# Sliding-window attention and a SiLU feed-forward on one core: the order of all work from a list scheduler, q and k in rows of 1.5 KB, v in four transfers a batch

## The chip, the cores and the metric

The kernel runs on one core of a Trainium2 chip. The metric is the device time of one execution in microseconds (us). A core has five engines that run side by side, each through its own instructions in their fixed order: PE (TensorE, matmuls and transposes), DVE (VectorE), ACT (ScalarE), POOL (GpSimd) and SP (SyncE, which here only issues transfers). PE's weight loads are shown as an engine of their own, PEld. An instruction waits at the head of its engine's queue for semaphores of the others, and everything behind it waits with it. Transfers (DMA) are issued by SP, ACT or POOL and then move by themselves.

## The reference

Attention over 8 batches, 8 heads, 576 positions and 64 values per head, where each position sees itself and the 63 before it; its output, as 4608 tokens of 512 values, goes through a feed-forward layer of width 2048.

```python
    scores = scale * np.matmul(q, k.transpose(0, 1, 3, 2))
    rel = pos[:, None] - pos[None, :]
    mask = (rel >= 0) & (rel < window)            # window = 64
    attn = np.exp(scores - max) / sum
    attn_out = np.matmul(attn, v)
    x = attn_out.transpose(0, 2, 1, 3).reshape(B * S, H * D)
    h = x @ w_in                                  # 4608x512 @ 512x2048
    g = h * (1.0 / (1.0 + np.exp(-h)))
    out = g @ w_out                               # 4608x2048 @ 2048x512
```

## The kernel before

**Attention.** The work is cut into 32 units `u` (one batch, two heads) and each unit into three groups `g` of three blocks of 64 positions, 96 groups in all. For a unit, `load_qk` brings q and k as 32-bit rows of 512 bytes (two positions), `cast` rounds them to 16 bits, `transposes` turns them on PE (six small matmuls for q, six for k) and copies the result from PSUM into `qbd` (two copies, one per head) and `kt` (one copy); these copies are called lifts below. `load_v` brings v in three transfers a unit, rounded on the way, and `fix_v` makes with two DVE copies the second alignment that the odd blocks need; these are called shifts.

A group is a chain through three engines: `scores` (three matmuls, then Exp on ACT at L168, then the mask on DVE at L169), `values` (three matmuls at L177, whose 65th column per head gives the sum; then on DVE a reciprocal at L184 and two multiplications at L187, together called the norm), `to_bridge` (three matmuls at L199 that bring the result back to the layout that the next layer reads, and a copy to `bridge` on ACT at L202).

**Feed-forward.** Tokens are taken in nine tiles of 512. `mm1` is the first layer: 16 output parts with four matmuls each (L226), each part followed by Silu on ACT (L233). `mm2` is the second layer: four blocks of 128 tokens with 16 matmuls each (L250), a copy on DVE (L238) and a store (L240). A tile of `mm1` has 64 matmuls of 512 columns and so has one of `mm2`.

**What sets the order.** The order is written out by hand. `interleave` runs the feed-forward as a stream and puts a step of other work behind every so many matmuls: in `mm1` after every sixth matmul one `bring_in` step (transposes, lifts and shifts of a later unit), in `mm2` after every third matmul one attention step (scores of one group, values of the group two steps back, `to_bridge` of the group four back). Tile 0's first layer is split into columns 0 to 191 and 192 to 511. `beside` says how many groups go beside each tile, 84 over tiles 0 to 7 (batch 0's 12 groups come before). Casts are on POOL from unit 4 on, between its v transfers; the first units' are on DVE and ACT. Lifts are shared by DVE and ACT in a fixed way. SP issues the q and k loads of later units and the stores.

**Buffers.** Four PSUM banks belong to the attention (`at_ps`) and four to the feed-forward (`moe_ps`).

## Time and profile before

| | |
|---|---|
| median of 3 runs | 395.9 us (395.88 to 396.58) |
| the profiled execution's own time, its span | 396.35 us, 394.6 us |
| mean granted TensorE clock | 0.989 |
| PE busy | 329.4 us, 83% |
| DVE busy | 232.9 us, 59% |
| ACT busy | 206.3 us, 52% |
| POOL busy (casts and issues of transfers) | 133.4 us, 34% |
| read from HBM, written | 36.70 MB, 9.44 MB |

Busy times are averages over stages with different limits. In the page's 40 slices PE is idle in the first two, at 4 to 8 tenths in the next two and between 7 and 9 later on; DVE changes between 9 and 4 tenths in the same slices in which PE changes between 7 and 9, and is idle from about 360 us on. The DMA engines are at 9 tenths in the first six and a half slices and seldom busy later. The chain that ended last is PE for 51% of the span, DVE for 32%, ACT for 6%.

### The profile page before, as it was taken

To read this page: it belongs to the slowest core of one execution; us is meant where nothing else is said; L and a number is where in the kernel's file an instruction comes from. 1 tells how busy PE (TensorE), PEld (TensorE's weight loads), DVE (VectorE), ACT (ScalarE), POOL (GpSimd) and SP (SyncE) were. 2 spreads that over 40 slices of the span, in tenths; PEclk is the share of its full clock that TensorE was granted. 3 is DMA by queue.
4 is the path that set the end of the run, shared out by engine and by line. 5 is a ranking of instruction groups with operands and counts; after the bars stand their busy time and mean duration, and the time that the engine had idled before them with its cause. 6 is when DMAs were issued, how large, how long until landed. Compare 5 with 4: busy or idle time off the path is not lost.

```text
span 394.6 us, 6598 instructions
## 1 busy us (share of the span) xinstructions
PE 329.4 (83%) x2423; PEld 180.0 (46%) x2464; DVE 232.9 (59%) x596; ACT 206.3 (52%) x410; POOL 133.4 (34%) x185
## 2 busy tenths in 40 slices
PE   0046896999989997899779978998799889989995
PEld 0035773545454554354435543545355544454442
DVE  0467979967584649664984485539944790093011
ACT  2066775545842774367445752585357645742710
POOL 8756999123900029200950077004900000000000
PEclk9999899899999999999999999999999999999999
DMA  9999999129901916382646456723710001001002
GB/s 190 166 213 250 119 209 174 9 17 272 120 27 71 250 10 64 71 213 54 65 51 185 109 57 86 201 67 43 71 55 0 30 27 55 0 28 69 13 27 80
DMA packets 83935, 37.65 MB, mean 95 GB/s; under 512 B 40256, under 2 KB 78656, under 8 KB 83904
## 3 DMA queue, kind: packets, MB, share of 16 engines
q0 software_dynamic: 45568, 11.28, 29.0%
q1 hardware_dynamic: 38336, 25.96, 24.4%
q8 instruction: 19, 0.31, 0.3%
q14 instruction: 12, 0.10, 0.1%
HBM read 36.70 MB, written 9.44 MB: 117 GB/s over the span
## 4 chain that ended last, share of the span: by engine, by line
PE 51%; DVE 32%; ACT 6%; issue 5%; POOL 2%; DMA 2%; DVEq 0%; ACTq 0%; POOLq 0%
PE ps L226 28%; PE ps L250 15%; DVE obd L187 13%; DVE e L169 7%; DVE rc L184 4%; PE pst L136 4%; ACT L168 2%; DVE ot L238 2%; PE pv L177 2%; DMA vv<-in_v_dram 2%; ACT e L168 2%; DVE qbd L143 2%; ACT gt L233 1%; POOL vv L75 1%; DVE vv L151 1%
## 5 line engine op out<-in xcount | busy, mean ns | idle before, releaser
L250 PE MATMUL ps<-w_out_sb,gt 128*128 128x512 bf16 x551 | 141.5, 381 | 1.3 <-ACT gt L233 0.3
L226 PE MATMUL ps<-bridge,w_in_sb 128*128 128x512 bf16 (+2 forms) x624 | 135.2, 359 | 0.9
L233 ACT ACTIVATE gt<-ps 128x512 bf16<-128x512 f32 (+2 forms) x160 | 84.6, 555 | 46.8 <-PE ps L226 45.3
L75 POOL DMA_DIRECT2D vv<-in_v_dram x64 | 49.1, 773 | 131.4 <-PE pv L177 90.6
L226 PEld LDWEIGHTS <-w_in_sb 128*128 128x128 bf16 x640 | 58.8, 99 | 51.9 <-issue 0.8
L169 DVE TENSOR_TENSOR e<-e,mask 128x384 bf16<-128x384 bf16 x96 | 43.0, 452 | 49.5 <-ACT e L168 47.1
L187 DVE TENSOR_TENSOR obd<-pv,rc 64x192 bf16<-64x192 f32 x192 | 68.2, 355 | 4.6
L250 PEld LDWEIGHTS <-gt 128*128 128x128 bf16 x576 | 49.4, 98 | 41.1 <-issue 1.0
L168 ACT ACTIVATE e<-sp 128x384 bf16<-128x384 f32 x96 | 44.7, 491 | 33.9 <-PE sp L162 33.8
L238 DVE COPY ot<-ps 128x512 f32<-128x512 f32 x36 | 24.6, 690 | 55.9 <-PE ps L250 55.3
L202 ACT CAST bridge<-op 128x192 bf16<-128x192 f32 x96 | 30.6, 318 | 45.6 <-PE op L199 44.3
L177 PE MATMUL pv<-vv,e 128*128 128x130 bf16 x288 | 33.8, 228 | 11.9 <-DVE e L169 6.8
L144 ACT COPY qbd<-pst 64x576 bf16<-64x576 bf16 x32 | 20.3, 633 | 40.3 <-DVE qbd L143 40.3
L199 PE MATMUL op<-twoi,obd 128*128 128x64 bf16 x288 | 25.1, 197 | 17.9 <-DVE obd L187 15.5
L162 PEld LDWEIGHTS <-kt 128*128 128x128 bf16 x288 | 25.2, 104 | 24.0 <-issue 2.9
L136 PE MATMUL pst<-ident,q_natb 96*128 96x96 bf16 x192 | 14.4, 214 | 26.0 <-DVE q_natb L126 26.0
L162 PE MATMUL sp<-qbd,kt 128*128 128x128 bf16 x288 | 33.2, 231 | 3.1 <-ACT kt L147 1.4
L147 DVE COPY kt<-pst 128x576 bf16<-128x576 bf16 x28 | 21.1, 755 | 18.3 <-PE pst L136 18.3
L177 PEld LDWEIGHTS <-e 128*128 128x128 bf16 x288 | 21.9, 101 | 20.9 <-DVE e L169 10.8
L199 PEld LDWEIGHTS <-obd 128*128 128x128 bf16 x288 | 15.7, 99 | 33.2 <-DVE obd L187 32.8
L143 DVE COPY qbd<-pst 64x576 bf16<-64x576 bf16 x32 | 24.0, 749 | 11.1 <-PE pst L136 11.0
L126 POOL CAST q_natb<-q_nat 96x768 bf16<-96x768 f32 x28 | 24.7, 881 | 13.3 <-DMA q_nat<-in_q_dram 13.3
(37 smaller groups left out, 188.8 us busy)
## 6 DMA issues: line engine op xcount, KB each, us to landing
out_dram<-ot SPq DMA_DIRECT2D x36, 256.0 KB, 2.1
q_nat<-in_q_dram SPq DMA_DIRECT2D x28, 288.0 KB, 6.1
k_nat<-in_k_dram SPq DMA_DIRECT2D x28, 288.0 KB, 6.1
vv<-in_v_dram POOLq DMA_DIRECT2D x64, 64.0 KB, 3.3
w_in_sb<-in_moe_w_in_dram POOLq DMA_DIRECT2D x8, 256.0 KB, 7.5
w_out_sb<-in_moe_w_out_dram POOLq DMA_DIRECT2D x8, 256.0 KB, 7.1
q_nat<-in_q_dram POOLq DMA_DIRECT2D x4, 288.0 KB, 8.8
k_nat<-in_k_dram POOLq DMA_DIRECT2D x4, 288.0 KB, 9.0
```

What stands on the lines that cost most here:

```text
L75: nc.gpsimd.dma_start(out=t[:, 1:9:2, hh * 65:hh * 65 + 64], in_=v[b, 2 * pj + hh, 0:512, :].rearrange("(c p) d -> p c d", p=128),)
L143: copies[0](out=d[0:64, 0], in_=src[0:64])
L162: nc.tensor.matmul(sp[:, x], lhsT=kt[i][:, t * 64:t * 64 + 128], rhs=qbd[i][:, :, t * 64:(t + 1) * 64], start=(x == 0), stop=(x == 2),)
L168: nc.scalar.activation(out=e, in_=sp, func=ACTF.Exp, scale=scale)
L169: nc.vector.tensor_mul(e, e, mask0 if g == 0 else mask)
L177: nc.tensor.matmul(pv[:, x, :], lhsT=e[:, x].rearrange("p h i -> p (h i)"), rhs=vv[i][:, 3 * g + x, :], start=(x == 0), stop=(x == 2),)
L187: nc.vector.tensor_mul(ob[p0:p0 + 64, :, p0:p0 + 64], pv[p0:p0 + 64, :, hh * 65:hh * 65 + 64], rc[p0:p0 + 64, :, hh:hh + 1].to_broadcast([ ...
L199: nc.tensor.matmul(op[:, x, :], lhsT=ob[:, x, :], rhs=twoi, start=(x == 0), stop=(x == 2))
L226: nc.tensor.matmul(ps[:, lo:hi], lhsT=w_in_sb[:, c, ft * 128:(ft + 1) * 128], rhs=bridge[c][:, t0 + lo:t0 + hi], start=(c == 0), stop=(c = ...
L233: nc.scalar.activation(out=gts[(j, ft)][:, lo:hi], in_=ps[:, lo:hi], func=ACTF.Silu)
L238: nc.vector.tensor_copy(out=ot, in_=ps)
L250: nc.tensor.matmul(ps[m], lhsT=gts[(j, f)][:, m * 128:(m + 1) * 128], rhs=w_out_sb[:, f, :], start=(f == 0), stop=(f == NFT - 1),)
```

## The change

The hand-written order goes. Every piece of work is added to a `Plan` with its class, the engines that may do it with a duration for each, and what it depends on. `Plan.run` then goes through the pieces in a model of the engines: whenever an engine is free it takes, in the order of `rank`, the first class whose next piece has its inputs and (for PE) a free PSUM bank; the instructions are emitted in that order. A piece of the kinds cast, lift, bridge copy or output copy may go to ACT or DVE, whichever is free. Scores are let through by `scores_may_run` only while the second layer runs with more than six matmuls left, or while the first layer has not its inputs yet.

Besides, a row of q and k now holds six positions (1.5 KB; 96 rows by two heads), k of batch 0 is issued by ACT, and v comes once per batch in four transfers of nine 128-row pieces, all issued by POOL, with two shifts per batch over 64x36x64 elements in place of eight over 64x512. `qbd`, `kt` and `vv` are kept per batch, two of each. Casts leave POOL altogether: by the order below 29 are on ACT and 35 on DVE. Tile 0's first layer is no longer split (64 matmuls fewer). All 96 groups are done by the fourth matmul of tile 5: beside tiles 1 to 4 stand 72 `values`, 69 `scores`, 71 `to_bridge` and 39 transposes of one q or k; tiles 5 to 8 have the feed-forward alone, but for one `to_bridge`.

```diff
+                for e in engines:
+                    if free[e] > now:
+                        continue
+                    for c in can[e]:
+                        q = self.queues[c]
+                        if head[c] == len(q):
+                            continue
+                        op = q[head[c]]
+                        if e not in op["us"]:
+                            continue
+                        if not self.done(op["deps"]) or (op["gate"] and not op["gate"]()):
+                            continue
+                        if op["pool"]:
+                            ok = [i for i, u in enumerate(self.banks[op["pool"]]) if self.done(u)]
+                            if not ok:
+                                continue
+                            op["bank"] = min(ok, key=lambda i: max(
+                                [u["seen"] for u in self.banks[op["pool"]][i]], default=0.0))
+                            self.banks[op["pool"]][op["bank"]] = op["until"]
+                        head[c] += 1
+                        us = op["us"][e]
+                        if op["table"] and op["table"] != table:
+                            table, us = op["table"], us + 1.28
+                        end = free[e] = now + us
+                        if op["dma"] is None:
+                            op["seen"] = end + op["lat"]
+                        else:
...
+                            pipe = max(pipe, end + 0.6) + op["dma"]
+                            op["seen"] = pipe + 1.4
+                        order.append((op, e))
+                        op["at"], op["cls"], op["by"] = now, c, e
+                        left -= 1
+                        moved = True
+                        heapq.heappush(events, end)
+                        heapq.heappush(events, op["seen"])
+                        break
+        for op, e in order:
+            op["fn"](e)
...
+    nats = [keep.tile([NR, 2, NM * D], FP32, name=f"nat{i}") for i in range(NN)]
+    natbs = [keep.tile([NR, NM, 128], BF16, name=f"natb{i}") for i in range(NNB)]
+    qbd = [keep.tile([128, NP, 2, S], BF16, name=f"qbd{i}") for i in range(NK)]
+    kt = [keep.tile([128, 64 + NP * S], BF16, name=f"kt{i}") for i in range(NK)]
+    vv = [keep.tile([128, H * NB + 1, D + 2], BF16, name=f"vv{i}") for i in range(NK)]
...
-    def load_v(u):
-        b, pj = divmod(u, NP)
-        t = vv[u % NK]
-        for hh in range(2):
-            nc.gpsimd.dma_start(
-                out=t[:, 1:9:2, hh * 65:hh * 65 + 64],
-                in_=v[b, 2 * pj + hh, 0:512, :].rearrange("(c p) d -> p c d", p=128),
-            )
...
+    p = Plan(
+        {name: len(b) for name, b in banks.items()},
+        rank=["one", "silu", "norm", "exp", "mask", "pv", "ot", "s", "bridge", "lift", "turn", "moe", "out",
+              "shift", "cast", "st", "ld0", "ld1", "dma"],
+    )
...
+    def load_qk(e, i, b, pj, kk):
+        queue[e].dma_start(
+            out=nats[i],
+            in_=(q, k)[kk][b, 2 * pj:2 * pj + 2].rearrange("h (p m) d -> p h (m d)", m=NM),
+        )
+
+    def load_v(b, part):
+        g0, g1 = part * 9, part * 9 + 9
         nc.gpsimd.dma_start(
-            out=t[64:128, 8, :].rearrange("p (h x) -> p h x", h=2)[:, :, 0:64],
...
+    def cast(e, i, w):
+        copies[e](
+            out=natbs[w].rearrange("p m (h d) -> p h m d", h=2),
+            in_=nats[i].rearrange("p h (m d) -> p h m d", m=NM),
+        )
...
+    def turn(op, w):
...
+    def lift_q(e, op, b, pj, hh):
+        r = slice(64 * hh, 64 * hh + 64)
+        copies[e](
+            out=qbd[b % NK][r, pj, hh].rearrange("x (p m) -> x p m", m=NM),
+            in_=at_bf16(op)[r].rearrange("x (m p) -> x p m", m=NM),
...
+    def lift_k(e, op, b, pj):
+        copies[e](
+            out=kt[b % NK][:, 64 + pj * S:64 + (pj + 1) * S].rearrange("x (p m) -> x p m", m=NM),
+            in_=at_bf16(op).rearrange("x (m p) -> x p m", m=NM),
...
+    def shift_v(b, hf):
+        t = vv[b % NK]
+        if hf:
+            nc.vector.tensor_copy(out=t[0:64, 2:H * NB + 1:2, 0:D], in_=t[64:128, 1:H * NB:2, 0:D])
         else:
-            d = kt[u % NK][:, 64:64 + S].rearrange("x (g p c) -> x g p c", g=3, c=2)
-            copies[0](out=d, in_=src)
...
+    def scores_may_run():
+        i = next((i for i in range(scores_may_run.i, len(moe)) if moe[i][0]["seen"] is None), None)
+        if i is None:
+            return True
+        scores_may_run.i = i
+        op, kind, rest = moe[i]
+        if kind == 1:
+            return rest == NFT * NDC and not p.done(op["deps"])
+        return rest > 6
+    scores_may_run.i = 0
...
+                           [ld, natb_free.get(w)])
+                nat_free[i] = ca
+                tu = p.add("turn", {"PE": 0.27}, None, [ca, c_ident] + busy, lat=0.1, pool="at")
+                tu["fn"] = lambda _, tu=tu, w=w: turn(tu, w)
+                natb_free[w] = tu
+                if kk:
+                    li = [p.add("lift", {"ACT": 0.64, "DVE": 0.75},
+                                lambda e, tu=tu, pj=pj: lift_k(e, tu, b, pj), [tu] + busy)]
+                else:
+                    li = [p.add("lift", {"ACT": 0.64, "DVE": 0.75},
+                                lambda e, tu=tu, pj=pj, hh=hh: lift_q(e, tu, b, pj, hh), [tu] + busy)
+                          for hh in range(2)]
+                tu["until"] = li
+                kq_done[(b, pj)] += li
+
...
+    def add_batch_v(b):
+        busy = pv_last.get(b - NK, []) + [c_vv[b % NK]]
+        lv = [p.add("dma", {"POOL": 1.0}, lambda _, part=part: load_v(b, part), busy, dma=2.7) for part in range(4)]
+        v_done[b] = lv + [p.add("shift", {"DVE": 0.8}, lambda _, hf=hf: shift_v(b, hf), lv) for hf in range(2)]
+
...
+                          kq_done[(b, pj)] + g_pv[n - NE:n - NE + 1] * (n >= NE), lat=0.1,
+                          gate=scores_may_run, pool="at")
+                s["fn"] = lambda _, s=s, pj=pj, g=g: scores(s, b, pj, g)
+                s_last[(b, pj)] = [s]
+                ex = p.add("exp", {"ACT": 0.5}, lambda _, s=s, n=n: expo(s, n), [s], table="exp")
...
-                if c == NDC - 1:
-                    if lo == 0:
-                        gts[(j, ft)] = g_pool.tile([128, TT], BF16, name="gt", tag="g")
-                    nc.scalar.activation(out=gts[(j, ft)][:, lo:hi], in_=ps[:, lo:hi], func=ACTF.Silu)
-                yield
...
-    for j in range(NTT):
...
-        for u in nxt:
-            load_v(u)
-            cast(u, "q", pcopy)
-            cast(u, "k", pcopy)
+                ot = n_ot[0] % NOT
+                n_ot[0] += 1
+                cp = p.add("out", {"DVE": 0.7, "ACT": 0.62}, lambda e, bank=bank[m], ot=ot: copy_out(e, bank, ot),
+                           [op, free_ot.get(ot)])
+                bank[m]["until"] = [cp]
+                free_ot[ot] = p.add("st", {"SP": 0.45}, lambda _, ot=ot, m=m: store(ot, j, m), [cp], dma=0.75)
+        free_gt.update(uses)
```

**DVE at the start.** Before, the clears of the buffers stand ahead of the first cast; `qbd`, `kt` and `vv` are a unit's buffers, and the L121 clears wait for v's transfers (DMASW).

```order
L120 MEMSET vv_106 64x65
L121 MEMSET vv_106 128x18 [waits DMASW7_49,DMASW0_49,DVE_49]
L117 MEMSET kt_99 128x32
L118 MEMSET qbd_91 64x288
L119 MEMSET qbd_91 64x288
L120 MEMSET vv_107 64x65
L121 MEMSET vv_107 128x18 [waits DMASW3_49,DMASW2_49,DVE_49]
L288 COPY twoi<-ident 64x64 [waits Pool_49]
L289 COPY twoi<-ident 64x64
L290 COPY mask_86<-mask 128x384 [waits Pool_49]
L291 MEMSET mask_86 64x64 [waits DVE_49]
```

After, the clears of two batches' buffers come first, and then lifts (L239, L245), casts (L221) and the first mask (L276); `at` is an attention PSUM bank, `nat` the loaded and `natb` the rounded q or k.

```order
L178 MEMSET kt_86 128x32
L179 MEMSET qbd_84 64x4x288
L180 MEMSET qbd_84 64x4x288
L239 COPY qbd_83<-at_145 64x576 [waits Activation_49]
L221 CAST natb_79<-nat_69 96x2x6x64 [waits DMAHW3_49]
L221 CAST natb_81<-nat_71 96x2x6x64 [waits DMAHW5_49]
L239 COPY qbd_83<-at_148 64x576 [waits PE_49]
L239 COPY qbd_83<-at_148 64x576
L245 COPY kt_85<-at_145 128x576 [waits PE_49]
L276 TENSOR_TENSOR e_89<-e_89,mask_65 128x384 [waits DVE_49,Activation_49]
L221 CAST natb_82<-nat_72 96x2x6x64 [waits DMAHW4_49]
```

The wait for v has moved from the clears to the first shift, 21 rows behind the last row shown.

**DVE in the middle.** Before, around the change from a first layer to a second one: lifts and shifts of the last two units, then masks and norms.

```order
L143 COPY qbd_94<-pst 64x576
L147 COPY kt_102<-pst 128x576
L151 COPY vv_110<-vv_110 64x4x2x64
L152 COPY vv_110<-vv_110 64x4x2x64
L143 COPY qbd_95<-pst 64x576
L147 COPY kt_103<-pst 128x576
L151 COPY vv_111<-vv_111 64x4x2x64
L152 COPY vv_111<-vv_111 64x4x2x64
L169 TENSOR_TENSOR e<-e,mask 128x384 x3
L184 RECIPROCAL rc<-pv 128x6
L187 TENSOR_TENSOR obd_112<-pv,rc 64x3x64 x2
L169 TENSOR_TENSOR e<-e,mask 128x384
```

After, in tile 1 around the same change (L288 and L291 are the norm, `ob` its output):

```order
L221 CAST natb_79<-nat_69 96x2x6x64
L239 COPY qbd_84<-at_147 64x576 x2
L221 CAST natb_80<-nat_70 96x2x6x64
L221 CAST natb_81<-nat_71 96x2x6x64
L276 TENSOR_TENSOR e_102<-e_102,mask_65 128x384
L276 TENSOR_TENSOR e_89<-e_89,mask 128x384
L288 RECIPROCAL rc_106<-at_145 128x6
L291 TENSOR_TENSOR ob_110<-at_145,rc_106 64x3x64 x2
L288 RECIPROCAL rc_103<-at_146 128x6
L291 TENSOR_TENSOR ob_111<-at_146,rc_103 64x3x64 x2
L276 TENSOR_TENSOR e_90<-e_90,mask 128x384
```

The casts of q and k stand now on DVE among the lifts, and masks and norms are no longer one after another by a fixed pattern.

**POOL.** Before, from tile 0 on, casts and v transfers take turns:

```order
L126 CAST q_natb<-q_nat 96x2x6x64 [waits PE_49]
L126 CAST k_natb<-k_nat 96x2x6x64 [waits PE_49]
L75 DMA vv_104<-in_v_dram 128x4x64 [waits DMASW0_49,PE_49]
L75 DMA vv_104<-in_v_dram 128x4x64 [waits DMASW1_49]
L79 DMA vv_104<-in_v_dram 64x2x64 [waits DMASW2_49,PE_49]
L126 CAST q_natb<-q_nat 96x2x6x64 [waits DMAHW0_49,PE_49,Pool_49]
```

After, POOL has only transfers; the first four of the third batch, which wait for PE to have read the first batch's v:

```order
L202 DMA vv_87<-in_v_dram 128x9x64 [waits DMASW0_49,DVE_49,PE_49]
L202 DMA vv_87<-in_v_dram 128x9x64 [waits DMASW1_49,PE_49]
L202 DMA vv_87<-in_v_dram 128x9x64 [waits DMASW2_49,PE_49]
L202 DMA vv_87<-in_v_dram 128x9x64 [waits DMASW3_49,PE_49]
L202 DMA vv_88<-in_v_dram 128x9x64 [waits DMASW4_49,DVE_49,PE_49]
```

The casts have left this queue.

## Rows read from the trace of the kernel before

**Rows 1.** Stretches: us, PE, PEld, DVE, ACT, POOL busy, PEclk, DMA, GB/s.

```profile
40.00:45.00 5.00, 3.79 (x37) 3.49 (x36) 4.60 (x16) 2.90 (x8) 4.17 (x7) 0.66 1.64 140
210.00:220.00 10.00, 9.89 (x75) 5.33 (x75) 6.41 (x12) 6.95 (x12) 0.00 (x0) 1.00 0.93 239
230.00:240.00 10.00, 7.38 (x68) 4.09 (x67) 9.25 (x25) 4.11 (x11) 10.00 (x15) 1.00 0.79 73
```

**Rows 2.** Chain of waits in order of time: start us, us, what.

```profile
89.25 1.24 PE ps L226 x5
...
167.98 1.08 PE ps L226 x5
...
209.84 1.08 PE ps L226 x5
...
362.98 6.47 PE ps L226 x30
...
390.65 0.69 DVE ot L238
```

**Rows 3.** Timeline around 206 to 232 us: start us, us, engine, line, instruction.

```profile
210.76 0.42 PE L136 MATMUL pst<-ident,q_natb 96*128 96x96 bf16 x6
...
212.31 0.42 PE L136 MATMUL pst<-ident,k_natb 96*128 96x96 bf16 x6
...
213.74 0.29 DVE L152 COPY vv<-vv 64x512 bf16<-64x512 bf16 x1
...
230.65 0.33 PE L177 MATMUL pv<-vv,e 128*128 128x130 bf16 x3
...
230.82 0.25 PE L199 MATMUL op<-twoi,obd 128*128 128x64 bf16 x3
...
230.91 0.81 PE L250 MATMUL ps<-w_out_sb,gt 128*128 128x512 bf16 x3
```

**Rows 4.** DVE groups of 310 to 327 us, where POOL is idle.

```profile
L187 DVE TENSOR_TENSOR obd<-pv,rc 64x192 bf16<-64x192 f32 x22 | 7.8, 355 | 0.5
L169 DVE TENSOR_TENSOR e<-e,mask 128x384 bf16<-128x384 bf16 x8 | 2.9, 358 | 0.2
L184 DVE RECIPROCAL rc<-pv 128x6 f32<-128x6 f32 x11 | 2.1, 194 | 0.3
```

**Rows 5.** Groups of the whole span by line and shape: busy us, mean ns.

```profile
L233 ACT ACTIVATE gt<-ps 128x512 bf16<-128x512 f32 x128 | 73.3, 597 | 45.9 <-PE ps L226 45.1
...
L168 ACT ACTIVATE e<-sp 128x384 bf16<-128x384 f32 x96 | 44.7, 491 | 33.9 <-PE sp L162 33.8
L169 DVE TENSOR_TENSOR e<-e,mask 128x384 bf16<-128x384 bf16 x96 | 43.0, 452 | 49.5 <-ACT e L168 47.1
...
L202 ACT CAST bridge<-op 128x192 bf16<-128x192 f32 x96 | 30.6, 318 | 45.6 <-PE op L199 44.3
...
L143 DVE COPY qbd<-pst 64x576 bf16<-64x576 bf16 x32 | 24.0, 749 | 11.1 <-PE pst L136 11.0
...
L144 ACT COPY qbd<-pst 64x576 bf16<-64x576 bf16 x32 | 20.3, 633 | 40.3 <-DVE qbd L143 40.3
...
L126 ACT CAST k_natb<-k_nat 96x768 bf16<-96x768 f32 x4 | 3.3, 831 | 3.4 <-DMA k_nat<-in_k_dram 3.4
...
L168 ACT ACT_TABLE_LOAD x8 | 10.3, 1283 | 0.1
...
L118 DVE MEMSET qbd<- 64x288 f32 x8 | 2.4, 298 | 0.0
...
L126 DVE CAST q_natb<-q_nat 96x768 bf16<-96x768 f32 x4 | 2.1, 537 | 0.1
```

**Rows 6.** Timeline of the start.

```profile
12.66 0.61 POOL L79 DMA_DIRECT2D vv<-in_v_dram  x1
...
20.22 0.66 PE L136 MATMUL pst<-ident,q_natb 96*128 96x96 bf16 x6 [20.22 <-DVE q_natb L126]
```

**Rows 7.** DMA issues of 2 to 20 us, last number us to landing.

```profile
vv<-in_v_dram POOLq DMA_DIRECT2D x4, 16.0 KB, 7.2
```

## What I predict, and how the numbers come about

> **What bounds the kernel now.** I read the chain of waits first, for the times at which the tiles begin, then the stretches, then the timeline of single instructions for PE's own pace, then the groups by line for what DVE and ACT have to do.
>
> PE's own pace. Tile 8 has nothing beside it: its first matmul starts at 362.98 and its last output copy at 390.65 [rows 2], so 128 matmuls take 27.67 us, 0.2162 each. In the first layer two pieces of transposes stand 1.55 us apart with six matmuls between [rows 3], so six transposes cost 1.55 - 6 x 0.2162 = 0.25. In a second layer the values begin at 230.65, the way back to the layout at 230.82 and the next matmul at 230.91 [rows 3]: 0.17 and 0.09. Scores are three matmuls like the values; I give them 0.17 as well. A group is 0.43.
>
> All of PE's work at this pace: 1152 x 0.2162 + 64 x 0.25 + 96 x 0.43 = 249.1 + 16.0 + 41.3 = 306.4 us. The first of it starts at 20.22 [rows 6], and behind the last output copy's start 394.6 - 390.65 = 3.95 us pass. So 394.6 - 20.2 - 306.4 - 3.95 = 64 us are PE standing still or at its lower clock. They lie in three places. (1) Before 20.22, because the first cast stands behind DVE's clears, which wait for v. (2) In batch 0's attention and tile 0: tile 1 begins at 89.25 [rows 2]. (3) In the second layers: the tile from 167.98 to 209.84 [rows 2] takes 41.86 us, and its own work (27.7, twelve groups 5.2, eight transposes 2.0) is 34.9, so 7.0 are lost. The stretches show where: from 230 to 240 us DVE is busy 9.25 of 10 and PE 7.38, from 210 to 220 DVE 6.41 and PE 9.89 [rows 1]. The attention's DVE work is all put beside second layers and DVE is the limit there, while in first layers it has time to spare.
>
> **The change part by part.** The terms are the start of tile 0, the start of tile 1, tiles 1 to 4 with all the attention left, tiles 5 to 8 with none, and the end.
>
> *Start of tile 0.* DVE's clears no longer wait. They run from about 0.9 us (an estimate): four of 64x1152, four times the 0.298 of 64x288 [rows 5], are 4.8; some 16 small ones, none taken above the 0.29 of a 512-element copy [rows 3] and put at 0.2, are 3.2. Then the order gives DVE, ahead of the first shift, 8 lifts of 0.749, 7 casts of 0.537 [rows 5] and 13 masks of 0.358 [rows 4]: 6.0 + 3.8 + 4.7. That is 23.6 without waits; for waits on PE and ACT in the first chains I add 0.9: 24.5. ACT's share ahead of it (7 casts of 0.831, 9 lifts of 0.633, 13 Exps of 0.491, a table of 1.283 [rows 5]) is 19.2, less than DVE's, so DVE is later. v must have landed by 24.5. In before its last transfer is issued at 12.66 and takes 7.2 [rows 6, 7], so it lands at 20; I take v as hidden. The two shifts have 4.5 times the elements of one before: at most 4.5 x 0.29 [rows 3] = 1.3 each, which I take. 27.1, the values 0.5 behind, then twelve norms of 0.194 + 2 x 0.355 = 0.904 [rows 4] with small gaps, 11.3: 38.9. One lift and a copy to `bridge` (0.318 [rows 5]) stand behind: tile 0 begins at 40.0.
>
> *Start of tile 1.* Tile 0's first layer is 13.85 + five transposes 1.25. PE is thinly used until then, and in before the stretch in which it came into steady work, 40 to 45 us, was granted 0.66 of full speed [rows 1]: between its two levels, 1.2 and 2.4 GHz, which costs (1 - 0.66) x 5 = 1.7. So 56.8. ACT: last Silu 0.8, table 1.28, twelve Exps 5.9: 64.8. DVE follows with the masks (0.133 shorter each than an Exp, so 1.6 of the two shifts' 2.6 are hidden), the last mask, a lift and the first values: 67.3. Twelve norms end at 78.6; way back and copy 0.7. Tile 1 begins at 79.5. PE's work by then would end at 77.2, so it stands 2.3 us. Before it was 89.25: only 10 us are won here.
>
> *Tiles 1 to 4.* PE: 4 x 27.7 + 39 x 0.25 + (69 + 72) x 0.17 + 71 x 0.09 = 110.8 + 9.75 + 24.0 + 6.4 = 150.9. DVE, by the order's counts and [rows 3 to 5]: 72 norms 65.1, 69 masks 24.7, 27 lifts 20.2, 23 casts 12.4, 10 shifts 13.0, 10 copies to `bridge` 3.2, 2 outputs 1.4 (0.69 each [rows 2]) = 140.0. ACT: 64 Silus of 0.597 are 38.2, 69 Exps 33.9, 62 copies to `bridge` 19.7, 31 lifts 19.6, 15 casts 12.5, 14 outputs at a Silu's length 8.4, 8 tables 10.3 [rows 5] = 142.6. PE is the longest of three, but DVE has 93% and ACT 94% of its time: nothing stands still without someone else noticing. How much PE waits is the term that no row shows. It is nothing if the three fit into one another, and 0.16 us for each of PE's attention pieces if they wait as in the tile of 41.86 us (7.0 over 12 x 3 + 8 = 44 pieces): 251 pieces, 40 us. The nearer row is the first layer's stretch, where pieces stand beside a DVE that is not full and PE keeps 9.89 of 10 [rows 1]; DVE is fuller here, so I take 5%, 8 us.
>
> *POOL.* Its casts go. A mask takes 0.358 where POOL is idle [rows 4] and 0.452 over the whole span [rows 5]; I have used 0.358. The Trainium skill (SBUF — State Buffer, section "SBUF: two separate sides") says that VectorE and GpSimd share a pair of ports that one of them holds for a whole instruction while the other "fully blocks". The mask rows agree with it. By that rule the casts, which are now DVE's, could hold POOL up in turn when it issues v; v is wanted a batch later, so this alone would leave the sum as it is.
>
> *Rows of 1.5 KB, four v transfers.* I cost them at nothing from tile 1 on: the attention works one to two batches ahead, and the loads go with it. If that cover were gone, a q would show its landing time once; the start has that case below.
>
> *Tiles 5 to 8 and the end.* 4 x 27.7 = 110.8, and 3.95 behind the last copy's start.
>
> Sum of the span: 79.5 + 150.9 + 8 + 110.8 + 3.95 = 353.2. The profiled execution took 396.35 for a span of 394.6, and the median is 0.45 below it, so +1.75 - 0.45: 354.5 us, 10% less than 395.9.
>
> **The rivals.**
>
> *A. The fixed order locks.* A list that is written by a model puts each PE piece where its input is just ready. If the real input comes later, all of PE's queue waits. At the 0.16 us a piece of before, tiles 1 to 4 lose 40 us: 345.2 + 40 + 1.3 = 386.5. For it: DVE and ACT have 6 or 7% to spare. Against: a late piece shifts the rest of the list as well, so that the same delay is not paid again, and Silu and Exp back to back can only be quicker than I counted.
>
> *B. v comes late at the start.* For it: q is issued by SP, k by ACT and v by POOL, behind which w_in is queued at once, and the loads of batch 1 come early too. If v lands at 30 to 35 in place of 24.5, tile 0 and all behind it move by 5 to 11: 360 to 366. Against: the bytes ahead of v are the same as before. The Trainium skill (DMA: Bandwidth & Descriptors, section "Queues, rings and completion order") has each DMA engine go round the queue rows that have work for it. No run here shows three rows at work. By that rule v would get a third of the turns in place of half, and its landing at 20 would become at most 30 (an estimate, 20 x 1.5): tile 0 later by 5.5, and 360 in all.
>
> *C. Slower than before.* The same place as A, but waits longer than before's: no spare time is left in DVE and ACT, and a mask that is late delays values, norm, way back and copy one after another. The point from which it decides: (395.9 - 346.5) / 251 = 0.197 us a piece. At 0.25 the sum is 346.5 + 63 = 409. For it: in before there are two steps between a group's scores and its values, here as few as the model wants. Against: before already paid 0.16 with DVE over its limit, and here DVE's demand is below PE's.
>
> That the order is not the planned one is no rival: it is read from the built program.
>
> **How the numbers follow.** My forecast, 354.5 with PE's wait between 0 and 20 us, has 71%; A (waits of 20 to 45) 13%; B 11%; C 3%; 2% for a gain lost in some other way that leaves no change. The range reaches down to 342 (no wait in tiles 1 to 4 gives 346.5, and 4 us less if the clears and first chains pack better than I added) and up to 370, which takes in B and the forecast with 20 us of waits and leaves out A's upper part and C. Chances: faster by over 0.2% 0.95, within 0.2% 0.02, slower 0.03; 0.2% is about what a measurement of this kernel can tell from no change.
>
> **What would show it.** First transposes before 10 us instead of at 20.22; tile 0's first matmul at 40 and tile 1's at 79.5; no idle PE in four tiles of 27.7 us each at the end; DVE and ACT at 9 tenths between 80 and 235 us with PE at 9 as well; masks of 0.36 us throughout. Wrong would be: PE at 7 tenths between 80 and 235 (A or C), the first shift waiting for a transfer (B), tile 5 beginning later than 255 us.

## The result and the profile after

The changed kernel takes 357.65 us (median of 4 runs, 356.06 to 358.78) beside 396.24 for the kernel before in the same session: a ratio of 0.902, 95% interval 0.899 to 0.906. The forecast was 354.5 in a range of 342 to 370. The profiled execution took 357.72 for a span of 355.8.

The first part of the page of after gives busy time and share of each engine; the rows below it are two of the 40 slices' rows, in tenths.

```profile
PE 323.2 (91%) x2358; PEld 178.4 (50%) x2400; DVE 193.4 (54%) x516; ACT 230.0 (65%) x448; POOL 46.7 (13%) x57
...
PE   1554699998999999999999999999999999999995
...
DVE  7966861679868989999978997791000000000000
```

PE went from 83% to 91% of a shorter span, and from the sixth slice to the last but one it is at 9 tenths, with one 8; before it changed between 7 and 9. DVE has no work from the 29th slice on: the attention is over by then, and the last third is the feed-forward alone.

The chain of waits of after, in order of time (start us, us, what), answers [rows 2]:

```profile
5.99 22.47 DMA vv<-in_v_dram
28.58 0.76 DVE vv L255
...
45.33 3.19 PE mp L305 x7
...
88.41 3.18 PE mp L305 x14
...
241.26 0.65 PE mp L305 x3
...
351.97 0.58 ACT ot L320
```

It begins with v: a transfer issued at 5.99 that lands after 22.5 us, then the first shift, then tile 0 at 45.33. From 88.41 on the pieces are PE's nearly without a break, and behind the last output copy's start 3.83 us pass.

The stretch of tiles 1 to 4, which before showed what [rows 1] show (PE at 7.38 of 10 where DVE was at 9.25), with the same columns:

```profile
86.23:241.09 154.86, 152.38 (x1356) 89.15 (x1381) 133.05 (x364) 127.22 (x264) 16.00 (x16) 1.00 0.55 103
```

PE is busy 98% of it, DVE 86%, ACT 82%.

Where the kernels begin their tiles, read from the timeline (the first first-layer matmul of each tile, us), with the medians; the rows below before and after are the experiments of the next section, and each of their ratios is to before in the same session. Some orders leave groups for tile 5, so tile 6 is the point at which all the attention is done.

| kernel | tile 0 | tile 1 | tile 6 | tiles 1 to 5 | median |
|---|---|---|---|---|---|
| before | 41.46 | 89.25 | 288.75 (not done) | | 396.24 |
| after | 45.33 | 86.23 | 268.84 | 182.6 | 357.65 |
| e1_hold | 36.74 | 85.69 | 270.88 | 185.2 | 359.67 |
| e7_rows512 | 41.22 | 81.41 | 264.30 | 182.9 | 353.35 |
| e8_vunit | 42.00 | 78.74 | 267.36 | 188.6 | 355.48 |
| e5_poolcast | 44.80 | 94.85 | 289.43 | 194.6 | 378.54 |
| e3_pvgate | 47.06 | 87.46 | 269.48 | 182.0 | 357.46 |
| e9_fixed | 45.51 | 88.34 | 287.84 | 199.5 | 376.39 |
| e6_blind | 45.56 | 89.37 | 313.57 | 224.2 | 402.16 |
| e13_low15 | 44.60 | 84.31 | 279.21 | 194.9 | 367.79 |
| e14_high15 | 45.22 | 86.11 | 268.32 | 182.2 | 357.15 |
| e4_nogate | 45.04 | 86.45 | 271.62 | 185.2 | 361.41 |
| e12_best | 40.73 | 76.90 | 260.46 | 183.6 | 349.83 |

After begins tile 1 only 3 us ahead of before. The rest of the 38.6 us is won behind it: from tile 1 to the start of the last output copy pass 301.4 us before [rows 2] and 265.7 after. Two questions are left: why the start is no better than that (v late?), and what keeps PE fed beside tiles 1 to 4.

### The profile page after: what moved, and what is told of

It is laid out like the page before. It is cut to its first block, busy times and chain, and to the rows that moved or that the text cites. A ratio compares the mean times of both kernels' runs of the same rounds, so it can differ in the third digit from the quotient of the medians.

```text
span 355.8 us, 6294 instructions
## 1 busy us (share of the span) xinstructions
PE 323.2 (91%) x2358; PEld 178.4 (50%) x2400; DVE 193.4 (54%) x516; ACT 230.0 (65%) x448; POOL 46.7 (13%) x57
## 4 chain that ended last, share of the span: by engine, by line
PE 75%; DVE 9%; DMA 6%; ACT 4%; issue 2%; POOL 1%; another core or an unknown queue 1%; DVEq 0%; ACTq 0%; POOLq 0%
PE mp L314 31%; PE mp L305 30%; DMA vv<-in_v_dram 6%; DVE ob L291 4%; PE at L267 4%; PE at L281 4%; PE at L232 3%; PE at L296 2%; ACT qbd L239 2%; DVE qbd L239 2%; DVE rc L288 1%; ACT g L311 1%; POOL vv L202 1%; DVE natb L221 1%
## 5 line engine op out<-in xcount | busy, mean ns | idle before, releaser
L314 PE MATMUL mp<-w_out_sb,g 128*128 128x512 bf16 x553 | 142.9, 379 | 0.9
L305 PE MATMUL mp<-bridge,w_in_sb 128*128 128x512 bf16 x557 | 133.9, 383 | 1.6 <-DVE ot L320 0.5
L311 ACT ACTIVATE g<-mp 128x512 bf16<-128x512 f32 x144 | 83.8, 598 | 25.8 <-PE mp L305 25.2
L314 PEld LDWEIGHTS <-g 128*128 128x128 bf16 x576 | 52.5, 98 | 41.7
L291 DVE TENSOR_TENSOR ob<-at,rc 64x192 bf16<-64x192 f32 x192 | 68.1, 355 | 4.6
L273 ACT ACTIVATE e<-at 128x384 bf16<-128x384 f32 x96 | 42.0, 500 | 11.9 <-PE at L267 11.5
L281 PE MATMUL at<-vv,e 128*128 128x130 bf16 x288 | 31.7, 229 | 9.4 <-DVE vv L255 5.1
L301 ACT CAST bridge<-at 128x192 bf16<-128x192 f32 x85 | 25.8, 319 | 21.7 <-PE at L296 20.8
L276 DVE TENSOR_TENSOR e<-e,mask 128x384 bf16<-128x384 bf16 x96 | 29.5, 353 | 15.9 <-ACT e L273 15.0
L267 PE MATMUL at<-qbd,kt 128*128 128x128 bf16 x288 | 30.0, 232 | 7.3 <-DVE qbd L239 3.9
L232 PE MATMUL at<-ident,natb 96*128 96x96 bf16 x384 | 28.2, 224 | 7.2 <-ACT natb L221 6.1
L239 DVE COPY qbd<-at 64x576 bf16<-64x576 bf16 x31 | 23.2, 751 | 10.3 <-PE at L232 5.8
L239 ACT COPY qbd<-at 64x576 bf16<-64x576 bf16 x33 | 20.9, 633 | 9.6 <-DVE qbd L239 5.4
L296 PE MATMUL at<-twoi,ob 128*128 128x64 bf16 x288 | 24.6, 200 | 2.0 <-ACT bridge L301 1.0
L221 ACT CAST natb<-nat 96x768 bf16<-96x768 f32 x29 | 23.8, 829 | 0.7 <-DMA nat<-in_q_dram 0.7
```

Of the source, the lines that this page charges most:

```text
L232: nc.tensor.matmul(pst[:, m], lhsT=natbs[w][:, m], rhs=ident[0:NR, 0:NR], is_transpose=True, start=(m == 0), stop=(m == NM - 1),)
L239: copies[e](out=qbd[b % NK][r, pj, hh].rearrange("x (p m) -> x p m", m=NM), in_=at_bf16(op)[r].rearrange("x (m p) -> x p m", m=NM),)
L267: nc.tensor.matmul(at_sp(op)[:, x], lhsT=kt[b % NK][:, pj * S + t * 64:pj * S + t * 64 + 128], rhs=qbd[b % NK][:, pj, :, t * 64:t * 64 + 6 ...
L273: nc.scalar.activation(out=es[n % NE], in_=at_sp(op), func=ACTF.Exp, scale=scale)
L276: nc.vector.tensor_mul(es[n % NE], es[n % NE], mask0 if g == 0 else mask)
L281: nc.tensor.matmul(at_pv(op)[:, x], lhsT=es[n % NE][:, x].rearrange("p h i -> p (h i)"), rhs=vv[b % NK][:, s:s + NB + 1:NB, 0:D + 1], star ...
```

## The experiments

### The start: why v lands at 28.5

**Batch 1's loads held back.** In SP's queue, ahead of batch 1's loads, a small store out of `vv` to a spare tensor `scrap`:

```diff
+    p.add("ld0", {"SP": 0.45}, lambda _: nc.sync.dma_start(out=scrap[0:1], in_=vv[0][0:1, 1:2 * 36:2, 0:D]), v_done[0][:4], dma=0.1)
```

> The kernel after, but SP's loads of batch 1's q and k wait until v of batch 0 has landed (a small transfer out of v stands ahead of them in SP's queue), and the scheduler knows it: 8 transposes in place of 15 stand before tile 0. Theory 1 (v is late because batch 1's loads take turns on the same DMA engines): the first shift starts between 21 and 25 us in place of 28.58, tile 0's first matmul at 38 to 42 in place of 45.33; the three more transposes beside tile 0 cost 0.8, the time is 352 to 356 us. Theory 2 (v is paced by its own queue and w_in behind it): the shift stays at 27 to 29, tile 0 at 43 to 46, and the time at 356 to 360.

Measured: 359.67 us, ratio to before 0.905 (0.903 to 0.908), 2 us slower than after and outside theory 1's time. The first shift of e1_hold starts at 22.71 and tile 0 at 36.74, 8.6 us earlier than after's. The timeline rows of after and of e1_hold (start us, us, then line and tiles; the bracket is the idle time ahead and what ended it):

```profile
28.58 0.76 DVE L255 COPY vv<-vv 64x2304 bf16<-64x2304 bf16 x1 [3.23 <-DMA vv<-in_v_dram]
```

and

```profile
15.50 0.86 SPq L452 DMA_DIRECT2D scrap<-vv  x1
...
22.71 0.76 DVE L255 COPY vv<-vv 64x2304 bf16<-64x2304 bf16 x1
```

The store, which waits for all of v, is issued at 15.50, so v has landed 13 us earlier than in after, and the shift at 22.71 waits only for DVE's own work. Batch 1's q and k were what made v late: theory 1 in this. But tile 1 begins at 85.69, where it did. The seven transposes of batch 1 that after does ahead of tile 0 now stand behind it, with their casts and lifts, and DVE, idle while it waits for them, has the same masks and norms to do before tile 1. The 8.6 us are given back between tiles 0 and 1: moving tile 0 is worth something only if batch 1's work doesn't move behind it. Tile 1 then starts at half pace (columns as in [rows 1]):

```profile
85.69:90.80 5.11, 5.11 (x30) 2.90 (x29) 3.61 (x9) 3.58 (x5) 0.03 (x1) 0.50 1.32 211
```

The granted clock reads 0.50 (1.2 GHz) from 77.2 to 90.8, behind a stretch in which PE waited for norms. Half of these 5.1 us is about what tiles 1 to 5 take more than in after (185.2 against 182.6).

**Rows of 512 bytes again.** The same order of instructions, only the loaded rows and the patterns that read them:

```diff
-            in_=(q, k)[kk][b, 2 * pj:2 * pj + 2].rearrange("h (p m) d -> p h (m d)", m=NM),
+            in_=(q, k)[kk][b, 2 * pj:2 * pj + 2].rearrange("h (g p c) d -> p (h g) (c d)", g=3, c=2),
```

> The kernel after with q and k loaded as rows of 512 bytes, as before the change; the order of all instructions is the same. Theory 1 (the rows matter at the start alone, where the DMA engines are full): a q of the start lands about 1 us later (6.0 in place of 4.9), v later by 1 to 3 us, tiles 1 to 4 as they were: 358 to 361 us. Theory 2 (the rows carry part of the gain): transfers are late beside tiles 1 to 4 too, and PE waits for lifts there: 364 us or more. Theory 3 (no part at all): 356 to 358.5.

Measured: 353.35 us, ratio 0.890 (0.888 to 0.893), so 4.3 us faster than after, which none of the theories had. The transfers of 2 to 30 us by queue (packets, MB, share of 16 engines) and the landing of v (count, KB each, median us from issue), of after:

```profile
q1 hardware_dynamic: 3520, 4.99, 67.7%
q0 software_dynamic: 5663, 1.09, 45.7%
...
vv<-in_v_dram POOLq DMA_DIRECT2D x4, 144.0 KB, 20.7
```

and of e7_rows512:

```profile
q1 hardware_dynamic: 7882, 3.93, 65.9%
q0 software_dynamic: 6166, 1.34, 51.4%
...
vv<-in_v_dram POOLq DMA_DIRECT2D x4, 144.0 KB, 14.2
```

In the same 28 us SP's queue (q1) moved 3.93 MB in place of 4.99, and POOL's (q0) 1.34 in place of 1.09. A v transfer lands after 14.2 us in place of 20.7, and the first shift starts at 24.97 with no wait. The rest follows: tile 0 is 4.1 earlier, tile 1 4.8, the span 4.6. The long rows make a q or k land a little sooner (median over the kernel 4.9 to 5.1 us, 5.5 with short rows), but all of that is hidden behind other work, while v, which shares the engines with them, is waited for. This part of the change costs 4 us.

**Shifts per quarter of v.** Each pair of shifts waits for one of v's four transfers, and values for the shifts of their heads:

```diff
-        v_done[b] = lv + [p.add("shift", {"DVE": 0.8}, lambda _, hf=hf: shift_v(b, hf), lv) for hf in range(2)]
+        for u in range(4):
+            v_done[(b, u)] = lv[:u + 1] + [p.add("shift", {"DVE": 0.25}, lambda _, hf=hf, u=u: shift_v(b, hf, u), [lv[u]]) for hf in range(2)]
```

> The kernel after with eight shifts of 64x576 a batch in place of two of 64x2304, each waiting for one of the four v transfers only, so that the first values wait for a quarter of v. Theory 1 (the four transfers land one after another): the first shift starts at 25 to 26 when DVE has got there, tile 0 at 42 to 44, the time 353 to 356. Theory 2 (the four land together, since they share the engines): the first shift stays at 27 to 28.5, the eight shifts cost DVE 0.2 to 0.5 us more a batch: 357 to 360.

Measured: 355.48 us, ratio 0.895 (0.892 to 0.898). Timeline rows of e8_vunit:

```profile
17.60 0.32 DVE L255 COPY vv<-vv 64x576 bf16<-64x576 bf16 x1
...
24.34 0.32 DVE L255 COPY vv<-vv 64x576 bf16<-64x576 bf16 x1 [0.21 <-DMA vv<-in_v_dram]
...
26.48 0.32 DVE L255 COPY vv<-vv 64x576 bf16<-64x576 bf16 x1 [1.46 <-DMA vv<-in_v_dram]
```

The quarters land one after another: theory 1, tile 0 at 42.0, though the first shift starts at 17.60 and not at 25. Tile 1 begins 7.5 us earlier, but tiles 1 to 5 take 6 more in this order, so of the 7.5 the median keeps 2.2.

### Tiles 1 to 4: what keeps PE fed

**Casts on POOL again**, for batches 2 to 7:

```diff
-                ca = p.add("cast", {"ACT": 0.84, "DVE": 0.56}, lambda e, i=i, w=w: cast(e, i, w),
+                ca = p.add("cast", {"POOL": 0.95} if b > 1 else {"ACT": 0.84, "DVE": 0.56}, lambda e, i=i, w=w: cast(e, i, w),
```

> The kernel after with the casts of batches 2 to 7 on POOL, as before the change (0.9 us each), in place of ACT and DVE. Theory 1 (POOL's casts slow DVE, but DVE and ACT have room beside tiles 1 to 4): masks go from 0.35 to 0.40 to 0.45 us while casts run, DVE and ACT lose 48 casts of 0.56 and 0.83, and the time stays within 356 to 360. Theory 2 (taking casts off POOL was part of the gain): PE waits for masks and norms again, 363 to 372. Theory 3 (ACT and DVE are the limit, so their relief counts): 350 to 355.

Measured: 378.54 us, ratio 0.951 (0.947 to 0.956): theory 2, and more than its 363 to 372. The group of the masks in e5_poolcast, and three timeline rows of its tile 0:

```profile
L276 DVE TENSOR_TENSOR e<-e,mask 128x384 bf16<-128x384 bf16 x96 | 38.4, 443 | 26.1 <-ACT e L273 25.1
```

```profile
53.05 3.05 POOL L202 DMA_DIRECT2D vv<-in_v_dram  x3 [1.48 <-DMA vv<-in_v_dram]
...
56.99 0.66 PE L232 MATMUL at<-ident,natb 96*128 96x96 bf16 x6 [7.96 <-POOL natb L221]
```

Two things are seen. A mask takes 443 ns in place of 353. And a cast in POOL's queue stands behind transfers that wait for something themselves; in the scheduler's model a transfer is taken only when nothing holds it up, so it put six transposes early in PE's queue, and PE stood 7.96 us for them. Tile 1 begins 8.6 us later, tiles 1 to 5 take 12 more. How much of this is the masks and how much the queue isn't separated.

**Casts off POOL, in the hand-written order** of before:

```diff
-    vcopy, acopy, pcopy = nc.vector.tensor_copy, nc.scalar.copy, nc.gpsimd.tensor_copy
+    vcopy, acopy, pcopy = nc.vector.tensor_copy, nc.scalar.copy, nc.scalar.copy
```

> The kernel before with one part of the change: the casts of units 4 to 31 on ACT in place of POOL, all else in the hand-written order. Theory 1 (before's waits beside second layers come from DVE being slowed by POOL): masks go from 0.45 to 0.36, twelve of them beside a second layer give 1.1 us a tile, and ACT, at 52%, takes 56 casts of 0.83: 385 to 392 us. Theory 2 (the hand-written order sets the waits, and the casts now stand in ACT's queue ahead of a Silu that PE waits for): 396 or more.

Measured: 397.04 us, ratio 1.001 (0.9995 to 1.003), although the masks went to 358 ns. The first waits of PE from 41 to 93 us in b1_castact (waiter, releaser, us in total, times, longest):

```profile
PE ps L226 <- ACT gt L233: 4.4, 1, 4.4
```

Eight casts in a row in ACT's queue now hold up the Silus behind them: tile 1 begins at 92.79, 3.5 us later than in before, and what the shorter masks give later (tile 5 at 248.07 beside 247.50) only makes that good. Both theories hold in part; taken alone in the old order, this edit gains nothing.

**Values only beside second layers:**

```diff
-                           [ma] + v_done[b] + g_back[n - NOB:n - NOB + 1] * (n >= NOB), lat=0.1, pool="at")
+                           [ma] + v_done[b] + g_back[n - NOB:n - NOB + 1] * (n >= NOB), lat=0.1, gate=scores_may_run, pool="at")
```

> The kernel after with values let through only when scores are: beside second layers and where a first layer has not its inputs yet, so that 11 to 14 of 18 groups a tile stand beside second layers as before the change, and the groups reach into tile 5. Theory 1 (what took PE's waits away is that groups now reach into first layers): DVE is over its limit beside second layers as in rows 1, PE loses up to 7 us in a tile again, 370 to 390 us. Theory 2 (the waits went with the casts on POOL and with copies that go to whichever of ACT and DVE is free): 356 to 361.

Measured: 357.46 us, ratio 0.901 (0.898 to 0.903), as after: theory 2. The gate moves little: 55 of the 72 values stand beside second layers, and in after 48 do already. It does give a pair to compare, second layers with 12 values beside them and no transposes, tile 3's of before and tile 4's of e3_pvgate (columns as in [rows 1]):

```profile
183.70:209.68 25.98, 20.91 (x171) 11.22 (x173) 19.00 (x51) 12.54 (x27) 15.15 (x20) 1.00 0.45 54
```

```profile
216.60:236.45 19.85, 19.63 (x186) 11.94 (x188) 17.59 (x58) 12.24 (x32) 3.99 (x4) 1.00 0.58 71
```

and the first and the last DVE rows of these groups in before:

```profile
186.39 1.12 DVE L169 TENSOR_TENSOR e<-e,mask 128x384 bf16<-128x384 bf16 x3 [4.78 <-ACT e L168]
...
206.10 0.69 DVE L238 COPY ot<-ps 128x512 f32<-128x512 f32 x1
```

So the number of groups beside a second layer doesn't make it long: 19.85 us in e3_pvgate, with PE busy 99% of it, and 25.98 in before. In before DVE works without a gap from 186.39 to 206.79, but has none of these groups' work in the 2.7 us ahead and the 2.9 us behind, while in e3_pvgate norms and masks run across the border between two layers.

**Copies with a fixed engine:**

```diff
-                br = p.add("bridge", {"ACT": 0.34, "DVE": 0.36},
+                br = p.add("bridge", {"ACT": 0.34},
...
-                cp = p.add("out", {"DVE": 0.7, "ACT": 0.62}, lambda e, bank=bank[m], ot=ot: copy_out(e, bank, ot),
+                cp = p.add("out", {"DVE": 0.7}, lambda e, bank=bank[m], ot=ot: copy_out(e, bank, ot),
```

> The kernel after with all output copies on DVE and all copies to bridge on ACT, as before the change. Theory 1 (the free choice of engine is what keeps PE fed): DVE has 0.69 more for each of 14 output copies beside tiles 1 to 4, second layers find it full, 363 to 372 us. Theory 2 (it matters little, since DVE and ACT have 5 to 7% to spare): 356 to 361.

Measured: 376.39 us, ratio 0.948 (0.945 to 0.951), beyond theory 1. The longest wait of DVE from 172 to 260 us in e9_fixed, and two stretches, up to its tile 4's start and around it:

```profile
DVE e L276 <- ACT e L273: 18.6, 2, 16.3
```

```profile
190.00:221.87 31.87, 27.74 (x289) 18.14 (x293) 26.91 (x85) 24.33 (x56) 4.00 (x4) 0.93 0.30 20
217.10:227.30 10.20, 8.16 (x42) 4.11 (x43) 7.38 (x16) 7.03 (x13) 0.00 (x0) 0.50 0.27 104
```

DVE stands 16.3 us for one Exp beside tile 4's first layer, so it isn't full over the whole time: without the choice the order has groups in bunches (20 values beside tile 3's second layer, none beside tile 4's first), and PE, ahead of tile 4, is busy 27.7 of 31.9. Behind that the granted clock reads 0.50 (1.2 GHz) up to 227.3, so tile 4's first 5.4 us run at half pace, some 2.7 of the 16.9 us that tiles 1 to 5 take more (an estimate). The free choice matters, but this run doesn't tell how much of it is DVE's 0.69 a copy and how much the poorer order that came out.

**Wrong durations in the scheduler.** Three lists for the same work, made with a DVE that is too fast or too slow. The edit of e13_low15; e6_blind has 0.19 and 0.48, e14_high15 0.43 and 1.09:

```diff
-                ma = p.add("mask", {"DVE": 0.37}, lambda _, n=n, g=g: masking(n, g), [ex, c_mask])
+                ma = p.add("mask", {"DVE": 0.31}, lambda _, n=n, g=g: masking(n, g), [ex, c_mask])
...
-                no = p.add("norm", {"DVE": 0.95}, lambda _, pv=pv, n=n: normal(pv, n),
+                no = p.add("norm", {"DVE": 0.81}, lambda _, pv=pv, n=n: normal(pv, n),
```

> The kernel after with the scheduler told half the length of a norm (0.48 in place of 0.95) and of a mask (0.19 in place of 0.37); the work is the same, its order is made for a DVE that does not exist: all groups stand before tile 4, 26 to 34 of them beside a tile. Theory 1 (the fixed order is only as good as the durations in the model, rival A): 24 groups a tile at 1.33 us of DVE, with lifts, casts and shifts, are over PE's 39 us a tile, PE waits in tiles 1 to 3, the time is 370 to 390 us. Theory 2 (the order corrects itself, since a late piece shifts the rest of the list as well): within 356 to 362.

> The kernel after with the scheduler told a norm of 0.81 in place of 0.95 and a mask of 0.31 in place of 0.37, 15% short. Theory 1 (an error of the durations turns into PE waits in proportion, 44.5 us for one of 50%): some 10 to 14 us more, 367 to 372 us. Theory 2 (DVE's 5 to 7% of spare time and the freedom of the order take up small errors): 356 to 361 us.

> The kernel after with the scheduler told a norm of 1.09 in place of 0.95 and a mask of 0.43 in place of 0.37, 15% long; 15% short gave 367.8. Theory 1 (only too short a duration costs: with too long a one a piece's input is ready before its turn comes, DVE has gaps, and seven or eight groups move into tile 5): 354 to 360 us. Theory 2 (any error of that size unbalances DVE and ACT, since the scheduler then gives too many lifts and copies to ACT): 363 to 372 us.

Measured: 402.16 us (ratio 1.014, 1.010 to 1.017), 367.79 (0.928, 0.925 to 0.931) and 357.15 (0.903, 0.900 to 0.905): theory 1 each time, for e6_blind beyond its 390. With durations at half, the scheduled kernel is slower than the hand-written one; with 15% short it loses 10 us; with 15% long it loses nothing. Waits of PE and a stretch of e6_blind, and tiles 1 to 4 of e13_low15:

```profile
PE at L296 <- DVE ob L291: 24.0, 64, 0.7
PE at L281 <- DVE ob L291: 7.9, 23, 0.7
```

```profile
170.00:210.00 40.00, 30.84 (x309) 18.17 (x313) 37.43 (x111) 23.43 (x48) 7.97 (x8) 1.00 0.58 66
```

```profile
84.31:251.59 167.28, 162.11 (x1399) 87.93 (x1397) 138.62 (x372) 128.54 (x263) 15.97 (x16) 1.00 0.51 99
```

The waits of PE's weight loads for a norm's output at the way back (us in total, times, longest), in tiles 1 to 4 of e13_low15, after and e14_high15:

```profile
PEld L296 <- DVE ob L291: 21.6, 53, 0.6
```

```profile
PEld L296 <- DVE ob L291: 6.2, 23, 0.6
```

```profile
PEld L296 <- DVE ob L291: 0.4, 1, 0.4
```

In e6_blind PE waits 64 times for a norm's output at the way back, 0.375 us each, and stands at 7 to 8 tenths where DVE is at 9: this is rival A, and in size rival C. The three rows of weight loads show the same wait grow as the norm in the list gets shorter. In after it stays small: the list's 0.95 for a norm is close to the 0.98 that the trace has from one norm to the next. A piece put too early in PE's fixed queue holds up all that stands behind it; one put too late only leaves DVE with a gap.

**Scores at any time:**

```diff
-            return rest == NFT * NDC and not p.done(op["deps"])
-        return rest > 6
+            return True
+        return True
```

> The kernel after with scores let through at any time, so that Exps fall among Silus: 38 table loads on ACT in place of 12. Theory 1 (ACT is nearly full beside tiles 1 to 4): 26 more loads of 1.283 are 33 us of ACT, most of it in tiles 1 to 4, where ACT has about 10 us to spare; PE waits for Silus and Exps, 365 to 380 us. Theory 2 (the scheduler puts the loads where ACT has nothing to do): 356 to 362 us.

Measured: 361.41 us, ratio 0.912 (0.909 to 0.914), 3.8 us slower than after: theory 2. The table loads in e4_nogate, ahead of Silus and ahead of Exps:

```profile
L311 ACT ACT_TABLE_LOAD x19 | 24.4, 1283 | 0.3
L273 ACT ACT_TABLE_LOAD x18 | 23.1, 1283 | 0.3
```

The 26 loads more than after's 12 are 33.4 us. ACT is busy 24.6 us more and DVE 8.0, to which the free choice moved copies; as the kernel is only 3.8 slower, most of it falls where the two had nothing to do.

### A version that is faster than both

Short rows, shifts per quarter, and output copies ranked ahead of lifts:

```diff
-        rank=["one", "silu", "norm", "exp", "mask", "pv", "ot", "s", "bridge", "lift", "turn", "moe", "out",
+        rank=["one", "silu", "norm", "exp", "mask", "pv", "ot", "s", "bridge", "out", "lift", "turn", "moe",
```

> Three edits together: rows of 512 bytes, shifts per quarter of v, and the class of output copies ranked ahead of lifts, so that a feed-forward bank comes free before DVE turns to lifts. Theory 1 (the gains at the start add up only to where DVE arrives, and the wait of tile 1's first layer for an output copy goes): tile 0 at 40 to 42, tile 1's first layer 4 to 6 us earlier than after's, 347 to 351 us. Theory 2 (v and rows are the same gain, and the rank gives nothing): 352.5 to 354.

Measured: 349.83 us (349.37 to 350.18), ratio 0.881 (0.879 to 0.884): theory 1 in the time and in tile 0's start, while tile 1 comes 9.3 us earlier than after's and not 4 to 6. The third edit comes from the start of tile 1 in after's timeline, where three lifts stand on DVE ahead of the output copies that free the bank:

```profile
85.06 2.30 DVE L239 COPY qbd<-at 64x576 bf16<-64x576 bf16 x3
...
87.67 1.28 DVE L320 COPY ot<-mp 128x512 f32<-128x512 f32 x2
...
88.41 3.18 PE L305 MATMUL mp<-bridge,w_in_sb 128*128 128x512 bf16 x14 [0.51 <-DVE ot L320]
```

and in e12_best the copies start on both engines before tile 1 does:

```profile
76.00 1.28 DVE L320 COPY ot<-mp 128x512 f32<-128x512 f32 x2
76.26 1.08 ACT L320 COPY ot<-mp 128x512 f32<-128x512 f32 x2
...
76.90 1.46 PE L305 MATMUL mp<-bridge,w_in_sb 128*128 128x512 bf16 x5
```

Tile 0 is half a microsecond earlier than in e7_rows512, tile 1 is 4.5 earlier, and tiles 1 to 5 take 183.6, so unlike in e8_vunit most of it is kept. What the rank gives by itself isn't shown: with the shifts alone, in e8_vunit, tile 1 began at 78.74.

## Why the prediction came out right, step by step

The total was 3.2 us short, and within that two errors went against each other: the start was predicted 6.7 us too early, tiles 1 to 4 were given 4 us too much. That the total is this close is luck in part: it is the forecast's number with a good part of rival B in it.

**Start of tile 0: 40.0 predicted, 45.33 measured.** DVE's sum of 24.5 ahead of the first shift came out near (its last mask there ends at 25.4), by errors that cancel: the clears end at 9.75 in place of 8.9, lifts, casts and masks are 13.3 us of work in place of 14.5, and the waits among them are 2.3 in place of 0.9. (The terms listed add up to 23.4, not to 23.6.) Taking v as hidden was the step that failed: DVE then waits 3.23. The 7.2 us that it went by are those of a transfer of 16 KB [rows 7]; one of 144 KB takes 20.7 here. The two shifts were over-priced by taking 4.5 times a small one: 0.76 and 0.83 in place of 1.3 each. Twelve norms took 11.8 in place of 11.3. Behind the last norm I had one lift and a copy; in the order stand transposes of batch 1 as well, whose banks are freed by lifts, and 2.9 us pass in place of 1.1. In all: 0.9 + 3.2 - 1.0 + 0.5 + 1.8 = 5.4.

Rival B thus came about, in place and cause, at two thirds of its lower price. What spoke against it, "the bytes ahead of v are the same as before", missed that the engines don't serve in the order of issue: batch 1's loads, most of them issued later, passed v (without them it has landed by 15.50, e1_hold). The Trainium skill (DMA: Bandwidth & Descriptors, section "Queues, rings and completion order") says that a DMA engine goes round the rows of queues that have work. The prediction had worked out from it a landing of at most 30 and a total of 360; the trace has 28.5 and 357.65, and agrees. The same section says that the engine changes rows only behind a whole packet; that longer rows on one queue take from the other is in line with it, and e7_rows512 shows it (14.2 against 20.7 us), but no run here shows in what turns the engines served the queues.

**Start of tile 1: 79.5 predicted, 86.23 measured.** Of the 6.7, 5.3 are tile 0's. From tile 0 to tile 1 40.9 us pass in place of 39.5. The first seven matmuls stand 0.43 us apart, from 45.33 to 48.31, and full pace is seen from 50.16 on: about 2 us more than at PE's pace, near the 1.7 that was put down for it.

**Tiles 1 to 4.** PE 150.9 plus a wait of 8 predicted, 154.86 measured: the wait is 4.0, half of what I took, and near the lower bound. DVE needed 133.1 in place of 140.0, since shifts were cheaper (twelve took 9.0, ten were put at 13.0) and masks back to back overlap (70 took 21.1, where 0.358 each would be 25.1). ACT needed 127.2 in place of 142.6: its groups add up to 137.5 (Silus 36.7 for 38.2, Exps 31.2 for 33.9), and the rest is overlap of instructions of different groups in the record. The groups for DVE, which answer to [rows 4] and [rows 5], are what was used:

```profile
L291 DVE TENSOR_TENSOR ob<-at,rc 64x192 bf16<-64x192 f32 x192 | 68.1, 355 | 4.6
...
L276 DVE TENSOR_TENSOR e<-e,mask 128x384 bf16<-128x384 bf16 x96 | 29.5, 353 | 15.9 <-ACT e L273 15.0
...
L288 DVE RECIPROCAL rc<-at 128x6 f32<-128x6 f32 x96 | 18.8, 196 | 7.2 <-PE at L281 4.2 <-ACT bridge L301 0.2
```

The reason that the prediction gave, that before loses time because DVE is the limit beside second layers, is borne out in part. DVE is full in before's second layers, but only for 20.4 of the 26.0 us shown under e3_pvgate, and as many groups fit beside a second layer of 19.85. So the loss isn't the place of the groups alone. Of the 7.0 us, 2.0 go with the casts on POOL: in b1_castact the second layers with 12 groups take 23.98 in place of 25.98,

```profile
186.70:210.68 23.98, 21.14 (x174) 11.22 (x173) 16.99 (x51) 14.09 (x31) 8.46 (x12) 1.00 0.50 58
```

and that run loses the gain again where casts hold up Silus. The other 5 us are argued from these rows, not shown by a run of their own: in the written order DVE comes in late and is done early in each second layer, and PE's matmuls are tied to the attention's steps between. What after needs, by the runs: durations not shorter than the real ones (e6_blind, e13_low15), casts away from POOL's queue (e5_poolcast), and, as far as e9_fixed tells, copies that may go to either engine.

**Masks.** 0.358 predicted, 353 ns measured, and 443 with casts on POOL. The Trainium skill (SBUF — State Buffer, section "SBUF: two separate sides") has VectorE and GpSimd share a pair of ports; these rows agree with it.

**Rows of 1.5 KB at nothing from tile 1 on.** Right: tiles 1 to 5 take 182.9 us in e7_rows512 and 182.6 in after. At the start, which was left to rival B, they cost 4.1 us, and B didn't name them.

**Tiles 5 to 8 and the end.** From tile 5 at 241.09 to the last copy at 351.97 are 110.9, 110.8 predicted; 3.83 behind it, 3.95 predicted; the rest outside the span 1.9 against 1.3.

**What would show it.** First transposes before 10 us: at 5.84. DVE and ACT at 9 tenths: 86 and 82%, PE 98. The first shift waiting for a transfer, named as the sign of B: seen.

## What to carry to other kernels

An order made by a scheduler is as good as the durations in its table: measure them in a trace, and round up rather than down (15% short cost 10 us here, 15% long nothing), for a piece that stands too early in a fixed queue stops all behind it while one that stands too late costs little. Check each start-up transfer that something waits for against all that is issued after it, on other queues as well, and keep the long rows away from the moment in which it is under way. A start that is earlier for one stage pays only if the work that the next stage waits for doesn't move behind it.

## What the runs showed of the hardware that was not expected

- Longer rows on one queue delay another queue's transfer: with q and k in rows of 1.5 KB a v transfer of 144 KB took 20.7 us to land, with 512 bytes 14.2, issued at the same time and in the same order.
- A copy of 64x2304 takes 0.755 us where 64x512 took 0.29 [rows 3]: 2.6 times for 4.5 times the elements.
- Behind stretches in which PE waited for norms, the granted clock fell to 0.50 (1.2 GHz) and stayed there into the next tile: for 5.1 us of tile 1 in e1_hold and 5.4 of tile 4 in e9_fixed.
- The first seven matmuls of tile 0 stand 0.43 us apart, twice PE's pace of 0.2162, while the granted clock of that stretch reads 1.00 (2.4 GHz):

```profile
45.00:49.00 4.00, 3.78 (x16) 1.75 (x15) 1.55 (x3) 3.59 (x5) 2.29 (x4) 1.00 1.88 177
```

In e7_rows512, whose order of instructions is the same, the stretch that begins with tile 0 reads 0.50 (1.2 GHz):

```profile
41.22:44.10 2.88, 2.88 (x10) 1.06 (x8) 1.38 (x4) 2.62 (x5) 1.00 (x1) 0.50 1.25 217
```

So after's first seven matmuls, at the same spacing, very likely ran at the lower level too, and the 1.00 that its record gives for this stretch isn't to be trusted. In the kernel before, the stretch that begins with tile 0 showed 0.66 [rows 1]. PE had been in use for 5.2 of the 7 us ahead of tile 0 in after.
